# Adding attention's mask by four fp32 products in quarters of the TensorE array instead of two over the whole array, with a shorter planned step

## The chip, the cores and the metric

The kernel runs on one core of one Trainium2 chip. The metric is the device time of one execution in microseconds (us); lower is better. TensorE (PE) multiplies, VectorE (DVE) and ScalarE (ACT) work element by element, GpSimd (POOL) helps in attention, and SyncE (SP) issues the DMAs. Each engine takes its instructions strictly in the order in which the program emits them, so an instruction that waits holds up everything behind it on its engine.

## The reference

The kernel computes windowed attention and two gated layers behind it, all in fp32. Cut to what matters:

```python
# q, k, v: (4 batches, 8 heads, 576 positions, 64)
scores = (1.0 / np.sqrt(64)) * np.matmul(q, k.transpose(0, 1, 3, 2))
rel = pos[:, None] - pos[None, :]
mask = (rel >= 0) & (rel < 64)               # each query sees itself and the 63 before it
scores = np.where(mask, scores, -1e9)
attn = softmax(scores)
x = np.matmul(attn, v) -> (2304 tokens, 512)
# first layer: 512 -> 1536 -> 512
y = (silu(x @ w_gate) * (x @ w_val)) @ w_out
# second layer: 512 -> 1024 -> 1024 -> 512
out = (((y @ w1) * (y @ w2)) @ w3) @ w_out2
```

## The kernel before

**Attention** runs in 24 steps, m = 0 to 23, and three more that drain it. A step takes two groups i of three blocks each; a block is 64 queries of two heads against 128 keys. `emit_S` makes the scores of the step in two PSUM banks S, one for each i. It first adds the mask: one product over the whole 128x128 array for each i, a scaled identity `identr` times the mask, 384 columns wide, in fp32r (one pass over the array for each product). Then come the 12 score products (3 blocks, 2 groups, 2 heads), 64x64 with 128 columns, in fp32. Each of those uses a quarter of the array: the rows go by the head h, the columns by `place(i, h)`. An fp32 product that is not a transpose shows as two records in the trace. The product over all rows writes the bank first (`start=True`), the scores add to it.

In one step PE then does, in this order: the mask and the scores of step m (S), transposes of later q and k (T), the product with v of step m-3 (PV) and the transposes of the probabilities of step m-2 (PT). ACT does the exponentials (`pexp`) and copies, DVE the maxima, the sums' reciprocals and the copies of the transposed probabilities (`ptt`), POOL the division.

**What fills the gaps.** The gated layer behind attention works on fp32 numbers split into a high and a low fp32r part. The splitting is small jobs: unpack a weight tile (DVE L188, L190, L194, ACT L192), form sums and differences for a Strassen-like scheme of seven products (`combine`, DVE L208), copy the high part (`cast`, ACT L200) and subtract it for the low part (`rest`, DVE L204). The names `w_g` and `w_v` are the parts of the first tiles of w_gate and w_val, `xo_10` to `xo_71` those of attention's output X for its first 768 tokens (the first digit is the product 1 to 7, the second the half).

A `Plan` orders these jobs while the program is written out. It keeps a clock and, for each engine, the time at which that engine becomes free. In attention, `filling` charges each engine with what a step costs it (DVE 2.75, ACT 3.2, POOL 2.6 us) and moves the clock forward by a planned step of 3.85 us. Jobs that fit below the clock are emitted into DVE's order there, and into ACT's and SP's a little later in the step (`during_attention`). What does not fit stays queued. It is emitted after attention, as more time passes or when a product asks for it (`plan.need`, which emits what the product lacks, at once). The 24 planned steps are the only place where attention hands out time for these jobs.

**Behind attention** step 24 writes the first three products of the first gated unit: `ala` (product 1, needs `xo_10`, `xo_11`), `gaa` (product 2, needs `xo_20`, `xo_21`) and `bea` (product 5, needs `xo_50`, `xo_51`), between PT and the next PV. ACT copies `ala` out into `ha`, DVE adds `gaa` to it, ACT applies silu. Step 25 and 26 write two products each, beside the last PV.

Of the kernel before, what the change touches and what calls it, by code (L numbers as in the profile page):

```python
# [7 lines left out]
F32 = mybir.dt.float32  # L8
F32R = mybir.dt.float32r
# [7 lines left out]
P = 128  # L17
# [15 lines left out]
def window_attention_moe_kernel(ctx: ExitStack, tc: tile.TileContext, q, k, v, w_gate, w_val, w_out, w1, w2, w3, w_out2, out):  # L33
    nc = tc.nc
# [7 lines left out]
    SUB = 3  # L42
    NSUB = NJ // SUB
# [11 lines left out]
    own = ctx.enter_context(tc.tile_pool(name="own", bufs=1))  # L55
    ps = ctx.enter_context(tc.tile_pool(name="ps", bufs=8, space=PSUM))

    def bank(name):
        return ps.tile([P, 512], F32, tag="bank", name=name)

    def slot(shape, dtype, name, counted=True):

        plan.slots -= counted
        return sl.tile(shape, dtype, tag="s", name=name)
# [90 lines left out]
    plan = Plan()  # L155
# [83 lines left out]
    class Weights(Doubles):  # L239
# [12 lines left out]
        def place(self, p, x):  # L252
            if self.count % 3 == 0:
                self.tile = slot([P, 3, 2, P], F32R, f"w_{self.name}_{p}{'hl'[x]}")
            self.ops[p, x] = self.tile[:, self.count % 3]
            self.count += 1
            return self.ops[p, x]
# [71 lines left out]
    def x_tile(tp, c):  # L329
        if (tp, c) not in X:  # L330
            X[tp, c] = slot([P, TP], F32, f"X{tp}_{c}")
        return X[tp, c]

    def attention(events, filling):
        if True:
            ident, identr = own.tile([P, P], F32, name="ident"), own.tile([P, P], F32R, name="identr")
            masktiles = [slot([P, 2, SUB, P], F32R, f"mask{x}", False) for x in range(2)]
            mask = [masktiles[0][:, 0], masktiles[0][:, 1], masktiles[1][:, 0]]

            units = [(b, pr) for b in range(B) for pr in range(PAIRS)]  # L340
# [2 lines left out]
            raw, vt, qT, kT, sc, pexp, ptp, ptt, stat = {}, {}, {}, {}, {}, {}, {}, {}, {}  # L343
# [50 lines left out]
            def place(n, h):  # L394


                return (h + n) % 2

            def emit_S(m):
                both = (2 * m, 2 * m + 1)  # L400
                for i in both:
                    sc[i] = bank(f"S{i}")[:, :SUB * P].rearrange("p (j k) -> p j k", j=SUB)
                    nc.tensor.matmul(sc[i], lhsT=identr, rhs=mask[i % NSUB], start=True, stop=False)
                for jj in range(SUB):
                    for i in both:
                        u, s = divmod(i, NSUB)
                        j = SUB * s + jj
                        keys = kT[u].rearrange("p (w n) -> p w n", n=64)

                        keys = keys[:, :2] if j == 0 else keys[:, j - 1:j + 1] if j % 2 else keys[:, j - 1:j + 1][:, ::-1]  # L410
                        for h in range(2):
                            r, c = 64 * h, 64 * place(i, h)
                            nc.tensor.matmul(sc[i][c:c + 64, jj, :], lhsT=qT[u][r:r + 64, 64 * j:64 * j + 64],  # L413
                                             rhs=keys[r:r + 64], start=False,
                                             stop=jj == SUB - 1)
# [100 lines left out]
            for m in range(NM + 3):  # L516

                u0, r = 2 * (m // 3), m % 3
# [9 lines left out]
                if m < NM:  # L528
                    emit_S(m)
# [15 lines left out]
                for x in parts:  # L545
                    evac_T(*x)

                filling(m, NM)
                if 1 <= m <= NM:
                    emit_norm(m - 1)  # L550
# [621 lines left out]
    def filling(m, NM):  # L1172
        if m < NM:
            for e, cost in (("DVE", 2.75), ("ACT", 3.2), ("POOL", 2.6)):
                plan.charge(e, cost)
            plan.advance(3.85, ("ACT", "POOL", "SP"))

    with tc.manual_schedule():
        plan.shut.add("POOL")
        attention(during_attention, filling)  # L1180
        plan.slots += ATTENTION
        plan.ahead = 1.0
        for _ in gate:
            pass
        for _ in project(rows, wos, events_p):
            pass
        on(events2, len(order2) - 6, lambda: make_to(w3s[-1]))
        begin_e, run_e = final(rows2)

        def put_all():  # L1190
            for j in by:
                plan.need(j)
            begin_e()
        on(events2, len(order2) - 4, put_all)
        for _ in gated(xop2, left2, order2, AF.Copy, h2d, events2):
            pass
        run_e()
# [30 lines left out]
```

## Time and profile before

| | |
|---|---|
| median of 3 runs | 848.73 us (847.08 to 850.55) |
| the profiled execution's own time | 848.98 us |
| its span, first to last instruction | 847.3 us |
| PE busy in the span | 822.9 us, 97% |
| attention: masks of steps 0 to 23 start at | 7.6 to 94.6 us |
| DVE busy, ACT busy, 44.02 to 91.50 us | 46.69 and 47.43 of 47.48 us |

The profile is of one execution. The clock column (PEclk) is the share of TensorE's full 2.4 GHz that was granted. A row of the timeline gives the start, the duration of the merged instructions together, the engine, line, operation and tiles, the count, and in brackets the idle time before it with what ended it. Starts are more reliable than ends on PE, whose ends are modelled, so the pace of PE is read here from one start to the next.

### The profile page before, as it was taken

Reading aid. Unit: us, or ns where it says so; the run is one execution under the profiler, and the core shown is the slowest. Engines: PE = TensorE matmul, PEld = TensorE weight load, DVE = VectorE, ACT = ScalarE, POOL = GpSimd, SP = SyncE. Lnnn points to the kernel's source line nnn. Section 1 sums busy time; section 2 is a strip of 40 time slices with the busy share of each in tenths; the row PEclk is TensorE's granted clock in tenths of the full one; section 3 lists DMA queues with packets and bytes.
Section 4 is the critical chain, followed back from the end, with each engine's and each line's share of the span. In section 5 each row is a group of like instructions: output and inputs, shape, how many; then the busy total and the mean of one; then the engine's idle time right before and its main releaser. Section 6 shows DMA issues by size and latency. Waiting matters only on the chain.

```text
span 847.3 us, 15757 instructions
## 1 busy us (share of the span) xinstructions
PE 822.9 (97%) x5870; PEld 791.6 (93%) x5870; DVE 642.5 (76%) x1364; ACT 451.2 (53%) x1188; POOL 60.8 (7%) x89
## 2 busy tenths in 40 slices
PE   7899878899999999999999999999999999999998
PEld 6688767899999999999999999999999998899998
DVE  4799779878688767976698585778788844788884
ACT  6799855564646464643563362544444423766452
POOL 3467600000000000000000000000000000000000
PEclk9999999999999999999999999999999999999999
DMA  9989200135255324689996851015555329623522
GB/s 203 219 174 211 72 1 38 46 121 189 97 207 191 142 91 162 224 301 385 374 307 183 227 200 50 1 75 161 149 167 170 121 83 353 214 78 124 173 75 75
DMA packets 147516, 136.29 MB, mean 161 GB/s; under 512 B 95088, under 2 KB 114288, under 8 KB 146416
## 3 DMA queue, kind: packets, MB, share of 16 engines
q1 hardware_dynamic: 147440, 135.29, 51.0%
q8 instruction: 46, 0.75, 0.4%
q14 instruction: 30, 0.25, 0.1%
HBM read 92.27 MB, written 42.99 MB: 160 GB/s over the span
## 4 chain that ended last, share of the span: by engine, by line
PE 80%; DMA 7%; DVE 4%; SPq 4%; ACT 4%; issue 1%; ACTq 0%; DVEq 0%
PE ala L583 14%; PE alb L583 13%; PE o L723 12%; PE beb L583 7%; PE bea L583 7%; PE al L947 6%; PE acc L881 5%; PE gaa L583 3%; PE gab L583 3%; PE be L947 3%; DMA wo<-wo 2%; SPq L350 2%; PE PV L466 2%; PE ga L947 2%; ACT pexp L427 1%; PE PT L446 1%
## 5 line engine op out<-in xcount | busy, mean ns | idle before, releaser
L723 PE MATMUL o<-ph,wo 128*128 128x384 f32 x576 | 146.7, 334 | 0.2 <-DVE X L710 0.2
L723 PEld LDWEIGHTS o<-ph,wo 128*128 128x128 f32 x576 | 104.2, 188 | 0.5 <-DVE X L710 0.5
L723 PE MATMUL o<-pl,wo 128*128 128x384 f32 x288 | 96.3, 334 | 0.1
L590 ACT COPY ha<-ala 128x384 f32<-128x384 f32 x90 | 42.7, 478 | 57.6 <-PE ala L583 51.2
L594 DVE TENSOR_TENSOR ha<-ha,bea 128x384 f32<-128x384 f32 x60 | 33.2, 553 | 35.8 <-PE bea L583 19.9
L723 PEld LDWEIGHTS o<-pl,wo 128*128 128x128 f32 x288 | 54.1, 188 | 0.4 <-DVE pl L204 0.4
L427 ACT ACTIVATE pexp<-S,stat 128x128 f32<-128x128 f32 x144 | 53.8, 432 | 0.0
L604 ACT ACTIVATE ha<-ha 128x384 f32<-128x384 f32 x54 | 28.3, 526 | 39.1 <-DVE ha L594 39.1
L204 DVE TENSOR_TENSOR hf<-h,hf 128x384 fp32r<-128x384 f32 x84 | 43.5, 553 | 5.6 <-ACT hf L200 5.6
L200 ACT CAST ph<-pl 128x768 fp32r<-128x768 f32 x36 | 29.2, 836 | 34.4 <-DMA pl<-h 27.7
L200 ACT CAST hf<-h 128x384 fp32r<-128x384 f32 x84 | 39.3, 513 | 13.0 <-DVE h L208 11.4
L204 DVE TENSOR_TENSOR pl<-pl,ph 128x768 fp32r<-128x768 f32 x36 | 33.5, 952 | 13.0 <-ACT ph L200 12.5
L437 POOL TENSOR_TENSOR pexp<-pexp,stat 128x384 f32<-128x384 f32 x48 | 38.7, 826 | 41.7 <-DVE stat L434 37.2
L590 ACT COPY c12b<-alb 128x384 f32<-128x384 f32 x30 | 14.4, 480 | 49.4 <-PE alb L583 49.3
L427 ACT ACTIVATION_READ_ACCUMULATOR pexp<-S,stat 128x1 f32 x144 | 38.3, 270 | 0.0
L594 DVE TENSOR_TENSOR c22b<-c22b,beb 128x384 f32<-128x384 f32 x30 | 16.6, 555 | 27.1 <-ACT c22b L590 27.0
L583 PE MATMUL ala<-xo,w_g_6l 128*128 128x384 f32 x90 | 29.6, 338 | 1.6 <-ACT xo L200 1.0
L420 DVE TENSOR_REDUCE stat<-S 128x3 f32<-128x384 f32 x48 | 24.4, 551 | 7.4 <-PE S L413 7.2
L583 PE MATMUL ala<-xo,w_g_1h 128*128 128x384 f32 x120 | 27.7, 345 | 1.7 <-ACT w_g_1h L200 1.7
L466 PE MATMUL PV<-ptt,v 128*64 128x64 f32 x576 | 22.8, 229 | 5.1 <-DVE ptt L452 2.3
L917 ACT COPY o<-al 128x256 f32<-128x256 f32 x36 | 13.4, 373 | 27.0 <-PE al L947 26.0
L466 PEld LDWEIGHTS PV<-ptt,v 128*64 128x64 f32 x576 | 19.5, 139 | 8.8 <-issue 3.8
(533 smaller groups left out, 2490.2 us busy)
## 6 DMA issues: line engine op xcount, KB each, us to landing
h<-ha SPq DMA_DIRECT2D x60, 384.0 KB, 3.2
pl<-h SPq DMA_DIRECT2D x36, 384.0 KB, 6.4
h<-h SPq DMA_DIRECT2D x24, 384.0 KB, 4.9
st_w<-in_moe_w_dram SPq DMA_DIRECT2D x8, 1024.0 KB, 6.3
st_g<-in_moe_w_gate_dram SPq DMA_DIRECT2D x6, 1024.0 KB, 6.3
st_v<-in_moe_w_val_dram SPq DMA_DIRECT2D x6, 1024.0 KB, 5.5
st_wo<-in_moe_w_out_dram SPq DMA_DIRECT2D x6, 1024.0 KB, 5.4
wo<-by_wo SPq DMA_DIRECT2D x12, 512.0 KB, 3.7
```

The source lines that it names most:

```text
L200: (eng.copy if eng is nc.scalar else eng.tensor_copy)(out=hi(), in_=src())
L204: return plan.job(lambda eng: eng.tensor_tensor(out=lo(), in0=src(), in1=hi().bitcast(F32), op=ALU.subtract), after, slots=slots, DVE=dve( ...
L427: nc.scalar.activation(out=pe[:, jj, :], in_=so[:, jj, :], func=AF.Exp, bias=st[:, 0, x, jj:jj + 1], accum_out=st[:, 1, x, jj:jj + 1])
L437: nc.gpsimd.tensor_tensor(out=pe, in0=pe, in1=st[:, 3, x, :].unsqueeze(2).to_broadcast([P, SUB, P]), op=ALU.mult)
L466: nc.tensor.matmul(pp[64 * h:64 * h + 64, 64 * (SUB * x + jj):64 * (SUB * x + jj) + 64], lhsT=vt[u][e][:, at, h, :], rhs=t[:, x, jj, c:c + ...
L583: nc.tensor.matmul(acc, lhsT=self.wt.ops[p, x][:, m, :], rhs=self.xs.ops[p, m][:, y, :], start=start and n == 0, stop=n == 5, skip_group_c ...
L590: nc.scalar.copy(out=out, in_=src)
L594: nc.vector.tensor_tensor(out=out, in0=x, in1=y, op=ALU.add)
L604: nc.scalar.activation(out=h, in_=src, func=func)
L723: nc.tensor.matmul(acc[m, x], lhsT=wos.tiles[i // 6][:, i % 6, :], rhs=rows[2 * tp + x].words(f, b), start=f == n == 0, stop=f == NF - 1 a ...
L881: nc.tensor.matmul(acc, lhsT=w3T[i][c // 3][:, x, (c % 3) * P:(c % 3) * P + P], rhs=zt[c, y], start=c == k == 0, stop=c == NI - 1 and k == 2)
L947: nc.tensor.matmul(acc, lhsT=self.xs.ops[p, m][:, x, t * P:t * P + P], rhs=right.ops[p, m, y], start=start and n == 0, stop=n == 3 * R - 1 ...
```

## The change

The mask is kept in fp32, and it is added by products of 64x64 in the same quarters as the scores: four for each step, two for each i, of 384 columns each. The planned step goes from 3.85 to 3.55 us; the charges of the engines stay.

```diff
-            ident, identr = own.tile([P, P], F32, name="ident"), own.tile([P, P], F32R, name="identr")
-            masktiles = [slot([P, 2, SUB, P], F32R, f"mask{x}", False) for x in range(2)]
+            ident, identr = own.tile([P, P], F32, name="ident"), own.tile([P, P], F32, name="identr")
+            masktiles = [slot([P, 2, SUB, P], F32, f"mask{x}", False) for x in range(2)]
...
                 for i in both:
                     sc[i] = bank(f"S{i}")[:, :SUB * P].rearrange("p (j k) -> p j k", j=SUB)
-                    nc.tensor.matmul(sc[i], lhsT=identr, rhs=mask[i % NSUB], start=True, stop=False)
+                for i in both:
+                    for h in range(2):
+                        r, c = 64 * h, 64 * place(i, h)
+                        nc.tensor.matmul(sc[i][c:c + 64], lhsT=identr[r:r + 64, r:r + 64], rhs=mask[i % NSUB][r:r + 64],
+                                         start=True, stop=False)
...
-            plan.advance(3.85, ("ACT", "POOL", "SP"))
+            plan.advance(3.55, ("ACT", "POOL", "SP"))
```

PE's order in one step in the middle of attention, before, from the last probability transposes to the first transposes of q (S_1221 and S_1223 are the two score banks, a count behind a row is the number of products):

```order
L446 MATMUL PT_1186<-ident,pexp_1098 128x128 x3
L403 MATMUL S_1221<-mask_131,identr 128x384
L403 MATMUL S_1223<-mask_130,identr 128x384
L413 MATMUL S_1221<-kT_1105,qT_1019 64x128 x2
L413 MATMUL S_1223<-kT_1198,qT_1108 64x128 x2
L413 MATMUL S_1221<-kT_1105,qT_1019 64x128 x2
L413 MATMUL S_1223<-kT_1198,qT_1108 64x128 x2
L413 MATMUL S_1221<-kT_1105,qT_1019 64x128 x2
L413 MATMUL S_1223<-kT_1198,qT_1108 64x128 x2
L376 MATMUL T_0_1240<-ident,rawq_1040 128x96 x3
```

The same place of the change (line numbers behind the edit are four higher):

```order
L450 MATMUL PT_1200<-ident,pexp_1111 128x128 x3
L406 MATMUL S_1231<-mask_131,identr 64x384 x2
L406 MATMUL S_1232<-mask_130,identr 64x384 x2
L417 MATMUL S_1231<-kT_1118,qT_1032 64x128 x2
L417 MATMUL S_1232<-kT_1212,qT_1121 64x128 x2
L417 MATMUL S_1231<-kT_1118,qT_1032 64x128 x2
L417 MATMUL S_1232<-kT_1212,qT_1121 64x128 x2
L417 MATMUL S_1231<-kT_1118,qT_1032 64x128 x2
L417 MATMUL S_1232<-kT_1212,qT_1121 64x128 x2
L376 MATMUL T_0_1252<-ident,rawq_1051 128x96 x3
```

The two whole-array products have become four of a quarter; nothing else of PE's order differs in attention.

ACT's order at the end of attention, before, from the last exponentials (the pexp rows) over the table load to the copies of the next PV:

```order
L200 CAST xo_31_2101<-X_3_776 128x384
L427 ACTIVATE pexp_2127,stat_2084<-S_2042,stat_2084 128x128 x3
L542 ACT_TABLE_LOAD
L542 ACTIVATE masks<-masks 128x1
L480 COPY X_2_1801<-PV_2106 128x384
L590 COPY ha_0_0_2137<-ala_0_2139 128x384
L604 ACTIVATE ha_0_0_2137<-ha_0_0_2137 128x384
L483 COPY X_2_1801<-PV_2168 128x192
```

And of the change, from the copy of X behind the table load to the same copy of PV:

```order
L484 COPY X_2_1810<-PV_2114 128x384
L200 CAST xo_10_2148<-X_0_455 128x384
L200 CAST xo_11_2151<-X_1_537 128x384
L594 COPY ha_0_0_2145<-ala_0_2147 128x384
L200 CAST w_v_6h<-st_v_461 128x256 x2
L200 CAST xo_20_2168<-X_2_709 128x384
L200 CAST xo_21_2171<-X_3_789 128x384
L608 ACTIVATE ha_0_0_2145<-ha_0_0_2145 128x384
L200 CAST w_v_6h<-st_v_461 128x256
L200 CAST w_v_6l<-st_v_461 128x256
L200 CAST xo_50_2188<-X_0_455 128x384
L200 CAST xo_51_2191<-X_1_537 128x384
```

Ten casts that stood among the steps of attention now stand here: two ahead of the copy of `ala`, four between it and silu, four behind silu.

DVE's order at the same place, before, from the last reciprocal of attention to the first copy of transposed probabilities behind it:

```order
L434 RECIPROCAL stat_2084<-stat_2084 128x6
L594 TENSOR_TENSOR ha_0_0_2137<-ha_0_0_2137,gaa_0_2147 128x384
L208 TENSOR_TENSOR X_1_528<-X_3_776,X_1_528 128x384
L208 TENSOR_TENSOR X_0_447<-X_2_698,X_0_447 128x384
L452 COPY ptt_2165<-PT_2119 128x384
```

And of the change, from the subtraction for xo_20 on:

```order
L204 TENSOR_TENSOR xo_20_2168<-X_2_709,xo_20_2168 128x384
L204 TENSOR_TENSOR xo_21_2171<-X_3_789,xo_21_2171 128x384
L598 TENSOR_TENSOR ha_0_0_2145<-ha_0_0_2145,gaa_0_2167 128x384
L204 TENSOR_TENSOR w_v_6l<-st_v_461,w_v_6h 128x256 x2
L204 TENSOR_TENSOR xo_50_2188<-X_0_455,xo_50_2188 128x384
L204 TENSOR_TENSOR xo_51_2191<-X_1_537,xo_51_2191 128x384
L204 TENSOR_TENSOR w_v_4l<-st_v_461,w_v_6h 128x256
L208 TENSOR_TENSOR X_0_455<-X_2_709,X_0_455 128x384
L208 TENSOR_TENSOR X_1_537<-X_3_789,X_1_537 128x384
L456 COPY ptt_2204<-PT_2127 128x384
```

Between the last reciprocal and the addition of `gaa` stand seven jobs where none stood (the five ahead of this piece are xo_10, xo_11, a part of w_v and two combinations), and between that addition and the copy of `ptt` seven where two stood. Further on the orders of all engines meet again after three more subtractions on DVE (for w_v_4l, xo_30 and xo_31) and two casts on ACT, and from there they are the same to the end. On SP two rows move: one load for later weights (`st_g`) goes behind ten later rows of loads of q, k and v, the other (`st_v`) to the end of attention's loads. On DVE the first unpacking of `st_v` (L188) stands one step later.

## Rows read from the trace of the kernel before

**Rows 1.** The page, head and part 1: the span, and PE's busy time and share.

```profile
span 847.3 us, 15757 instructions
PE 822.9 (97%) x5870; PEld 791.6 (93%) x5870; DVE 642.5 (76%) x1364; ACT 451.2 (53%) x1188; POOL 60.8 (7%) x89
```

**Rows 2.** Windows: length, busy of PE, PEld, DVE, ACT, POOL; then clock, DMA, GB/s.

```profile
44.02:91.50 47.48, 47.48 (x837) 39.48 (x835) 46.69 (x118) 47.43 (x223) 32.52 (x44) 1.00 0.88 189
96.00:118.00 22.00, 16.53 (x159) 14.48 (x159) 12.59 (x28) 11.11 (x37) 7.06 (x10) 0.92 0.01 1
118.00:165.00 47.00, 39.97 (x217) 37.01 (x216) 40.89 (x86) 28.16 (x65) 0.00 (x0) 1.00 0.09 34
200.00:700.00 500.00, 499.18 (x2876) 498.06 (x2876) 379.08 (x759) 234.41 (x485) 0.00 (x0) 1.00 0.52 176
```

**Rows 3.** Timeline of PE over one step in mid-attention.

```profile
61.65 0.87 PE L446 MATMUL PT<-ident,pexp 128*128 128x128 f32 x6
62.28 0.60 PE L403 MATMUL S<-mask,identr 128*128 128x384 f32 x2
62.81 0.89 PE L413 MATMUL S<-kT,qT 64*64 64x128 f32 x24
63.63 0.71 PE L376 MATMUL T<-ident,rawk 96*128 96x96 f32 x6
64.52 0.92 PE L466 MATMUL PV<-ptt,v 128*64 128x64 f32 x24
66.00 0.42 PE L403 MATMUL S<-mask,identr 128*128 128x384 f32 x1
```

**Rows 4.** Timeline of the weight loads (PEld) in the same step.

```profile
62.81 0.64 PEld L413 LDWEIGHTS S<-kT,qT 64*64 64x64 f32 x24 [0.25 <-issue]
63.62 0.53 PEld L376 LDWEIGHTS T<-ident,rawk 96*128 96x128 f32 x6 [0.17 <-issue]
```

**Rows 5.** Timeline of PE in stretches 0.035 us long, at 62.97 and at 63.08.

```profile
62.81 0.45 PE L413 MATMUL S<-kT,qT 64*64 64x128 f32 x8
62.81 0.56 PE L413 MATMUL S<-kT,qT 64*64 64x128 f32 x12
```

**Rows 6.** Timeline of PE in the gated layer: fp32r products of 384 columns.

```profile
136.02 1.20 PE L583 MATMUL beb<-xo,w_v_5h 128*128 128x384 f32 x6
137.06 1.20 PE L583 MATMUL alb<-xo,w_v_6h 128*128 128x384 f32 x6
```

**Rows 7.** Timeline of PE in attention's first half: its three waits.

```profile
24.28 0.36 PE L376 MATMUL T<-ident,rawq 96*128 96x96 f32 x2 [2.02 <-DMA rawq<-in_q_dram]
34.45 1.03 PE L466 MATMUL PV<-ptt,v 128*64 128x64 f32 x24 [0.50 <-DVE ptt L452]
38.75 0.94 PE L466 MATMUL PV<-ptt,v 128*64 128x64 f32 x24 [0.58 <-ACT pexp L427]
```

**Rows 8.** Timeline of DVE there.

```profile
33.23 0.43 DVE L188 TENSOR_SCALAR st_v<-st_v 128x512 int32<-128x512 int32 x1 [1.78 <-DMA st_v<-in_moe_w_val_dram]
```

**Rows 9.** Timeline of PE at the end of attention and behind it.

```profile
94.59 0.60 PE L403 MATMUL S<-mask,identr 128*128 128x384 f32 x2
95.11 0.89 PE L413 MATMUL S<-kT,qT 64*64 64x128 f32 x24
102.32 2.06 PE L583 MATMUL ala<-xo,w_g_1h 128*128 128x384 f32 x6
104.22 0.51 PE L583 MATMUL gaa<-xo,w_g_1h 128*128 128x384 f32 x2
107.63 0.94 PE L466 MATMUL PV<-ptt,v 128*64 128x64 f32 x24 [1.17 <-DVE ptt L452]
```

**Rows 10.** Timeline of ACT at the same place.

```profile
101.50 0.46 ACT L480 COPY X<-PV 128x384 f32<-128x384 f32 x1
104.41 0.48 ACT L590 COPY ha<-ala 128x384 f32<-128x384 f32 x1 [2.46 <-PE ala L583]
```

**Rows 11.** Timeline of DVE at the same place.

```profile
105.53 0.55 DVE L594 TENSOR_TENSOR ha<-ha,gaa 128x384 f32<-128x384 f32 x1 [4.82 <-PE gaa L583]
106.93 1.01 DVE L452 COPY ptt<-PT 128x384 f32<-128x384 f32 x2
```

**Rows 12.** Timeline in the gated layer: casts in a row, subtractions in a row.

```profile
131.37 3.00 ACT L200 CAST xo<-X 128x384 fp32r<-128x384 f32 x7
118.93 1.96 DVE L204 TENSOR_TENSOR xo<-X,xo 128x384 fp32r<-128x384 f32 x4
```

## The prediction

> **What bounds the kernel now.** I read the page first: PE is busy for 97% of the span [rows 1]. Next the windows by stage [rows 2]: from 200 us on PE runs without a gap worth naming (499.18 of 500 us), so whatever the first 165 us lose or win comes out at the end unchanged; nothing behind it can take it up. That leaves two stretches. In mid-attention, 44.02 to 91.50 us, PE is busy for all of the 47.48 us, but DVE and ACT are at 98% and 100% too, so the share alone doesn't say who sets the step. The timeline does: in a whole step [rows 3] no PE row has an idle time, and PE's weight loads wait only for "issue" [rows 4], which is PE changing its tiling and no other engine. So the step is PE's: masks start at 62.28 and 66.00, and over the 13 steps from 44.02 to 91.50 the mean is 3.65 us. The second stretch, 96 to 165 us, is the other way round: PE is idle for 5.5 us of 22 and 7.0 us of 47 [rows 2], and the waits name ACT and DVE [rows 9 to 11].
>
> **The mask on PE.** From start to start, the two fp32r products take 0.53 us, the scores 0.82 [rows 3]. Of the first, 0.25 is the change of tiling ahead of the scores, of the second 0.17 is the change ahead of T [rows 4]; so scores alone stream for 0.65 us. They are 12 products of 128 columns, 1536 columns in fp32, each in a quarter. The new mask is 4 products of 384 columns: the same 1536 columns, type and quarters, with the same order over the quarters. Does all of that run four abreast? In two stretches 0.11 us apart the records begun since 62.81 are 8 and 12 [rows 5]: four records start every 0.107 us, one for each quarter, and 0.107 us is 128 columns at two clocks each at 2.4 GHz. So I price the mask at 0.64 us. Cross-check of the old one: six fp32r products of 384 columns take 1.04 us from start to start [rows 6], 0.17 each, so two stream for 0.35 and the rest of the 0.53 is the switch. A switch is not saved: scores follow the mask without one, but the mask now follows the probability transposes (whole array, 61.65 to 62.28 [rows 3]) with one, which I take at 0.17. New block: 0.17 + 0.64 = 0.81 against 0.53, **+0.28 us a step**. Bounds: if a record in a quarter streamed one column a clock, as fp32r does, the mask would take 0.32 + 0.17 = 0.49 (-0.04); if only two quarters ran at once, 1.28 + 0.17 = 1.45 (+0.92). The scores are the nearest row by far (same type, same quarters), so I take the middle value.
>
> The Trainium skill speaks against that ("TensorEngine Tiling (Array Packing)", Restrictions and Gotchas, Gotcha 1): different row tiles cannot access one PSUM bank at the same time. By that rule the two heads of a group i, which sit in different row halves and write one S bank, would take turns, and the price would be the +0.92 above. The trace disagrees: the score products of [rows 5] have just this layout and start in fours.
>
> **Where the 0.28 lands.** Steps 0 to 4: nothing; the transposes of step 4 wait 2.02 us for a load of q that lands at 24.28 whatever PE does [rows 7], more than 5 x 0.28. Steps 5 to 8 (27.1 to 44.0 us): +1.1 us on PE, but PE has two waits there, 0.50 for DVE's `ptt` and 0.58 that the profile gives to ACT [rows 7]. The first goes back to DVE standing 1.78 us at L188 for the load of `st_v` [rows 8], with `ptt` behind it. The change puts L188 a step later, and puts less filler on both engines, so I count both waits as gone: +0.1 in all (bounds 0 and +1.1). The 13 steps to 91.50: 13 x 0.28 = +3.6; DVE and ACT, which might be next to bind, carry less per step than before. The last step before the final scores is 94.59 - 91.50 = 3.09 us long [rows 2, 9], where PE has about 2.85 to do, so it grows by 0.04, and the last mask adds 0.28. **Attention: +4.0 us** (bounds +3 and +5.2).
>
> **The work put off.** The shorter planned step takes 24 x 0.30 = 7.2 us of planned time from the jobs. In the orders, ten casts and twelve DVE jobs more than before now stand between the last exponentials and the copy of `ptt` that PV of step 25 needs. A row of casts runs at 0.42 us each (seven in 3.00, the last 0.51), a row of subtractions at 0.47 (four in 1.96) [rows 12]. I use before's times; attention's +4.0 comes on top.
> - ACT copies X at 101.50 in both [rows 10], as the last exponentials and the table load are not moved. `xo_10` then starts at 101.92 and ends at 102.43, `xo_11` at 102.85; DVE's low parts follow at 103.0 and 103.45. `ala` started at 102.32 and took 1.90 to the next start [rows 9], slow; it now starts at 102.45 and meets its low parts on the way, so it ends about 0.1 late, and ACT copies it at 104.5 instead of 104.41.
> - ACT then casts two parts of w_v, `xo_20` and `xo_21` before anything else: `xo_20` is there at 104.5 + 3 x 0.42 + 0.51 = 106.3, `xo_21` at 106.7, low parts at 106.8 and 107.25. `gaa`, which ran at 104.22 without a wait, now ends near 107.6, and DVE adds it at 107.8 instead of 105.53 [rows 11]: +2.2.
> - silu on ACT waits for that addition, and behind silu wait two more casts of w_v, `xo_50` and `xo_51`. Silu starts at 108.35; `xo_50` is there at 108.35 + 3 x 0.42 + 0.51 = 110.1, `xo_51` at 110.55, the low parts at 110.65 and 111.1. `bea` needs them and ends near 111.6.
> - DVE, at its low part of `xo_51` until 111.1, has a part of w_v and two combinations (3 x 0.47 less overlap, 1.3) ahead of `ptt`, which so starts near 112.3, against 106.93. PV of step 25, which waited for `ptt` until 107.63 [rows 9, 11], starts near 113.0: **+5.3 us**. Bounds: +4.5 if the 256-column casts of w_v are quicker than the 0.42 of the 384-column ones; +7 if PE, idle between those products, gets the low clock for `gaa` and `bea` as well (`ala` shows it: 0.32 for each product against 0.17 in [rows 6]).
>
> From there PE, ACT and DVE have the old order again, with three more subtractions on DVE (1.4 us) and two more casts on ACT (0.8) before 128 us. DVE is idle for 6.1 of 47 us there [rows 2] and takes part of it; PE waits for both engines, so I take +0.7 (bounds 0 and 1.4). The moved loads cost nothing: they are weights for the second set of tiles, whose L188 is not in attention, and no load of attention is queued behind `st_v`.
>
> **The sum**: 4.0 + 5.3 + 0.7 = +10.0 us on the profiled execution's 848.98 us (span 847.3 and 1.7 around it), 0.25 above the median: 859.0 us, 1.2% more.
>
> **The rivals.**
> 1. Quarters cost no more than the whole array. For it: the low bound of the mask, which no fp32 row here reaches; against: [rows 5]. Attention then gives -0.04 x 18 steps and the two waits, -1.7 in all, the rest stays: 848.98 - 1.7 + 6.0 = 853.3.
> 2. Only two quarters at once. For it: the page's rule; against: the scores. 18 x 0.92 - 1.0 = +15.6 and 6.0: 870.6.
> 3. Faster: DVE and ACT set the step, not PE. At 98% and 100% busy they might, if PE's back-to-back starts only follow their pace. Each step would then shed the 0.30 us of jobs that the plan no longer puts in: 18 x 0.30 = -5.4. The put-off jobs cost nothing if they fit into the idle time behind attention: DVE has 22 - 12.59 = 9.4 us of it, ACT 10.9 [rows 2], for some 5 us each. That gives 843.6. It decides only from the point where PE has a gap in each step that the longer mask can use; [rows 3, 4] show none, and the put-off jobs stand in a chain with PE, not beside it.
>
> **How the numbers follow.** Forecast 0.77, with its own range from its bounds, +7.5 to +13.6: 856.5 to 862.6. Rival 1 0.10, rival 2 0.06, rival 3 0.07. A change under 0.5% (4.2 us) can't be told from none by this measurement. Faster: rival 3 mostly, 0.06. Same: most of the rest of rival 3, half of rival 1, 0.07. Slower: 0.87. The range, 853.2 to 864, holds the forecast with some room above for a longer low clock and nearly all of rival 1's upper half.
>
> **What would show it.** Right: in mid-attention the scores start 0.64 us behind the mask, and masks stand 3.93 us apart in the mean instead of 3.65, with an "issue" idle ahead of the mask's weight loads and none ahead of the scores'; DVE and ACT idle in attention; PE waits on ACT's `xo_20` and `xo_50` casts behind attention, `ptt` of step 25 about 5 us later after the last scores; from 200 us on the same rows, shifted by 10. Wrong: masks under 3.7 or over 4.2 us apart (the price of a quarter), or `gaa` starting without a wait (the chain behind silu).

## The result, and the profile after

| | before | after |
|---|---|---|
| median of 4 runs each | 849.13 us (847.08 to 850.55) | 862.01 us (861.46 to 863.58) |
| ratio, 95% interval | | 1.0142 (1.0111 to 1.0172) |
| the profiled execution's own time, span | 848.98, 847.3 us | 862.04, 860.3 us |

The change costs 12.9 us; 859.0 was forecast, with 853.2 to 864.0 as the range. The page's head and part 1 and the windows of the changed kernel, which answer [rows 1, 2]:

```profile
span 860.3 us, 16045 instructions
PE 834.2 (97%) x6014; PEld 795.0 (92%) x6014; DVE 641.3 (75%) x1364; ACT 454.1 (53%) x1188; POOL 59.1 (7%) x89
```

```profile
43.16:94.26 51.10, 51.10 (x913) 39.91 (x912) 39.97 (x108) 46.13 (x214) 31.41 (x44) 1.00 0.78 169
96.00:118.00 22.00, 14.41 (x158) 10.52 (x156) 15.70 (x35) 12.95 (x48) 7.59 (x11) 0.79 0.00 1
118.00:165.00 47.00, 40.03 (x220) 36.21 (x218) 36.98 (x76) 25.94 (x60) 0.00 (x0) 0.92 0.12 40
200.00:700.00 500.00, 500.00 (x2886) 499.88 (x2885) 384.38 (x771) 239.64 (x495) 0.00 (x0) 1.00 0.53 179
```

PE has no gap in these 13 steps of attention, as before, and none from 200 to 700 us, where it had 0.82 us of them [rows 2]; DVE and ACT now have idle time in attention (39.97 and 46.13 of 51.10). New is the clock column: 0.79 and 0.92 in the two stretches behind attention, 0.92 and 1.00 before. One step of PE in mid-attention, and its weight loads, for [rows 3, 4]:

```profile
61.89 0.87 PE L450 MATMUL PT<-ident,pexp 128*128 128x128 f32 x6
62.70 0.88 PE L406 MATMUL S<-mask,identr 64*64 64x384 f32 x8
63.39 0.83 PE L417 MATMUL S<-kT,qT 64*64 64x128 f32 x24
64.16 0.71 PE L376 MATMUL T<-ident,rawk 96*128 96x96 f32 x6
66.70 0.55 PE L406 MATMUL S<-mask,identr 64*64 64x384 f32 x4
```

```profile
62.70 0.21 PEld L406 LDWEIGHTS S<-mask,identr 64*64 64x64 f32 x8 [0.17 <-ACT X L487]
63.07 0.15 PEld L417 LDWEIGHTS S<-kT,qT 64*64 64x64 f32 x4 [0.17 <-issue]
```

From start to start the mask takes 0.69 us (its four products show as 8 records, two each), the transposes ahead of it 0.81, where they took 0.63, and the scores behind it 0.77, where they took 0.82. PE behind attention, which answers [rows 9]:

```profile
98.07 0.83 PE L417 MATMUL S<-kT,qT 64*64 64x128 f32 x24
105.04 0.44 PE L587 MATMUL ala<-xo,w_g_1h 128*128 128x384 f32 x1 [1.10 <-ACT xo L200]
109.27 1.28 PE L587 MATMUL gaa<-xo,w_g_1h 128*128 128x384 f32 x2 [1.61 <-ACT xo L200]
114.07 2.56 PE L587 MATMUL bea<-xo,w_g_2l 128*128 128x384 f32 x6 [2.24 <-ACT xo L200]
116.96 1.55 PE L470 MATMUL PV<-ptt,v 128*64 128x64 f32 x24 [0.33 <-DVE ptt L456]
```

ACT and DVE at the same place, for [rows 10, 11]:

```profile
107.69 0.48 ACT L594 COPY ha<-ala 128x384 f32<-128x384 f32 x1 [2.29 <-PE ala L587]
108.70 0.92 ACT L200 CAST xo<-X 128x384 fp32r<-128x384 f32 x2
112.45 0.52 ACT L608 ACTIVATE ha<-ha 128x384 f32<-128x384 f32 x1 [2.83 <-DVE ha L598]
113.51 0.92 ACT L200 CAST xo<-X 128x384 fp32r<-128x384 f32 x2
```

```profile
109.25 1.03 DVE L204 TENSOR_TENSOR xo<-X,xo 128x384 fp32r<-128x384 f32 x2 [0.99 <-ACT xo L200]
111.86 0.55 DVE L598 TENSOR_TENSOR ha<-ha,gaa 128x384 f32<-128x384 f32 x1 [1.59 <-PE gaa L587]
116.26 1.01 DVE L456 COPY ptt<-PT 128x384 f32<-128x384 f32 x2
```

PE now waits for the casts ahead of `ala`, `gaa` and `bea`, and four windows of the changed kernel show what else is new there:

```profile
110.00:112.00 2.00, 1.82 (x5) 1.31 (x5) 0.41 (x2) 0.00 (x0) 0.00 (x0) 0.50 0.00 0
114.00:116.00 2.00, 1.93 (x5) 1.63 (x6) 1.95 (x5) 0.43 (x2) 0.00 (x0) 0.50 0.00 0
126.00:128.00 2.00, 2.00 (x8) 2.00 (x7) 0.00 (x0) 0.48 (x1) 0.00 (x0) 0.50 0.00 0
143.00:146.00 3.00, 3.00 (x11) 3.00 (x11) 1.97 (x5) 2.41 (x6) 0.00 (x0) 0.50 0.00 0
```

The granted clock is 0.50 (1.2 of 2.4 GHz) in three stretches that follow waits of PE, the first of which the first two windows show; in it the six products of `bea` are busy for 2.56 us where six such products have 1.20 in [rows 6].

Where the 12.9 us lie, by landmarks on PE's timeline of both kernels: the last scores start 2.96 later (95.11 to 98.07); from there to PV of step 25 it takes 18.89 us where it took 12.52, +6.37; from there to `ala` of the seventh unit (the one that waits for ACT's `w_g_1h`) 56.21 where it took 51.71, +4.50. The rows of that `ala`, before and after:

```profile
159.34 1.44 PE L583 MATMUL ala<-xo,w_g_1h 128*128 128x384 f32 x6 [1.73 <-ACT w_g_1h L200]
173.17 1.44 PE L587 MATMUL ala<-xo,w_g_1h 128*128 128x384 f32 x6 [1.71 <-ACT w_g_1h L200]
```

The three add up to 13.83; the spans differ by 13.0, since PE's 0.82 us of gaps from 200 to 700 us are gone. The forecast had 4.0, 5.3 and 0.7.

### The profile page after: what moved, and what is told of

Read it like the earlier page. It is cut to its first block, busy times and chain, and to the rows that moved or that the text cites. A ratio compares the mean times of both kernels' runs of the same rounds, so it can differ in the third digit from the quotient of the medians.

```text
span 860.3 us, 16045 instructions
## 1 busy us (share of the span) xinstructions
PE 834.2 (97%) x6014; PEld 795.0 (92%) x6014; DVE 641.3 (75%) x1364; ACT 454.1 (53%) x1188; POOL 59.1 (7%) x89
## 4 chain that ended last, share of the span: by engine, by line
PE 88%; SPq 3%; DVE 3%; DMA 3%; ACT 2%; issue 1%; DVEq 0%; ACTq 0%
PE o L727 17%; PE ala L587 14%; PE alb L587 13%; PE beb L587 7%; PE bea L587 7%; PE al L951 6%; PE acc L885 5%; PE gab L587 4%; PE gaa L587 3%; PE be L951 3%; PE PV L470 2%; SPq L350 2%; PE ga L951 2%; PE S L406 1%; PE PT L450 1%; PE T L376 1%
## 5 line engine op out<-in xcount | busy, mean ns | idle before, releaser
L431 ACT ACTIVATE pexp<-S,stat 128x128 f32<-128x128 f32 x144 | 51.8, 394 | 0.0
L431 ACT ACTIVATION_READ_ACCUMULATOR pexp<-S,stat 128x1 f32 x144 | 33.5, 233 | 0.0
L204 DVE TENSOR_TENSOR xo<-X,xo 128x384 fp32r<-128x384 f32 x42 | 22.6, 574 | 8.9 <-ACT xo L200 8.9
L417 PEld LDWEIGHTS S<-kT,qT 64*64 64x64 f32 x576 | 18.9, 137 | 8.5 <-issue 7.3
L587 PEld LDWEIGHTS ala<-xo,w_g_1h 128*128 128x128 f32 x120 | 21.1, 188 | 5.7 <-DVE xo L204 2.1
```

The costliest lines, as they stand in the source:

```text
L204: return plan.job(lambda eng: eng.tensor_tensor(out=lo(), in0=src(), in1=hi().bitcast(F32), op=ALU.subtract), after, slots=slots, DVE=dve( ...
L431: nc.scalar.activation(out=pe[:, jj, :], in_=so[:, jj, :], func=AF.Exp, bias=st[:, 0, x, jj:jj + 1], accum_out=st[:, 1, x, jj:jj + 1])
L587: nc.tensor.matmul(acc, lhsT=self.wt.ops[p, x][:, m, :], rhs=self.xs.ops[p, m][:, y, :], start=start and n == 0, stop=n == 5, skip_group_c ...
```

## The experiments

Each kernel ran beside the kernel before on the same chip. The last three were on a chip where that one took 851.02 us instead of some 849.8, so the ratio is what compares.

| run | mask | planned step | median us | before, same chip | ratio (95%) |
|---|---|---|---|---|---|
| e1_mask_alone | fp32, quarters | 3.85 | 857.19 | 849.90 | 1.0077 (1.0051 to 1.0104) |
| e2_step_alone | fp32r, whole | 3.55 | 856.61 | 849.90 | 1.0079 (1.0058 to 1.0101) |
| e5_quarters_bf16 | bf16, quarters | 3.85 | 850.38 | 849.90 | 1.0000 (0.9982 to 1.0018) |
| e7_busy_gaps | fp32, quarters | 3.55 | 862.70 | 849.90 | 1.0156 (1.0132 to 1.0181) |
| e8_step_370 | fp32r, whole | 3.70 | 851.34 | 849.62 | 1.0021 (1.0003 to 1.0038) |
| e9_busy_gaps2 | fp32, quarters | 3.55 | 858.81 | 849.62 | 1.0116 (1.0093 to 1.0140) |
| e10_before_busy | fp32r, whole | 3.85 | 848.11 | 849.62 | 0.9978 (0.9962 to 0.9993) |
| e11_bf16_380_busy | bf16, quarters | 3.80 | 847.99 | 849.62 | 0.9986 (0.9970 to 1.0001) |
| e12_x_first | fp32, quarters | 3.55 | 865.35 | 851.02 | 1.0181 (1.0152 to 1.0210) |
| e13_mask_alone_busy | fp32, quarters | 3.85 | 854.26 | 851.02 | 1.0040 (1.0021 to 1.0058) |
| e14_step_alone_busy | fp32r, whole | 3.55 | 857.20 | 851.02 | 1.0074 (1.0052 to 1.0097) |

**Mask alone and step alone.** The first is the change without its last line, the second is the kernel before with that line:

```diff
-            plan.advance(3.85, ("ACT", "POOL", "SP"))
+            plan.advance(3.55, ("ACT", "POOL", "SP"))
```

> The four fp32 products in quarters, with the planned step left at 3.85 us. By the theory on record the mask makes PE's step 0.28 us longer (3.65 to 3.93 us over the 13 steps of mid-attention, +3.6), the last mask adds 0.28, steps 5 to 8 up to 1.1, and the orders behind attention stay as before: +4 to +5 us, 853 to 854. If the whole loss were the mask's, 862; if it were the plan's alone, 849.

> The planned step of 3.55 us, with the two fp32r products kept. By the theory PE's step stays at 3.65 us (attention shorter by 1 us at most, from the waits of the first half), the put-off jobs cost some 6 us up to the PV of step 25, and the low clock and later waits some 3 more: +8 to +9, 857 to 858. If the whole loss were the mask's, 849. If DVE and ACT set the step of before, 18 steps give back 0.30 us each and the time is near 852.

The two losses, 0.77% and 0.79%, add up to that of the change, 1.42%, within their intervals. So both halves lose, each by about the same. The step alone lost 6.7 us by its median, a little under its expectation of 8 to 9. PE's timeline of the mask alone, the scores of steps 9 and 23:

```profile
44.75 0.83 PE L417 MATMUL S<-kT,qT 64*64 64x128 f32 x24
98.97 0.83 PE L417 MATMUL S<-kT,qT 64*64 64x128 f32 x24
```

And of the step alone:

```profile
44.71 0.89 PE L413 MATMUL S<-kT,qT 64*64 64x128 f32 x24
94.73 0.89 PE L413 MATMUL S<-kT,qT 64*64 64x128 f32 x24
113.99 1.55 PE L466 MATMUL PV<-ptt,v 128*64 128x64 f32 x24 [0.33 <-DVE ptt L452]
```

From the scores of step 9 to those of step 23 it is 54.22 us with the quarters, 50.02 without, where before has 50.57 (44.54 to 95.11). All six runs with fp32 quarters give 54.21 or 54.22, with either planned step: the mask's price there is 3.65 us against the kernel before, and 4.20 against the step alone. A step given 0.30 us less filler is shorter by 0.04 us in the mean (0.55 in 14 steps, half of it in the last), so the third rival (DVE and ACT set the step) falls. What is put off shows in the last row: 19.26 us from the last scores to PV of step 25, against 12.52, with the mask of before.

The mask alone was over its expectation by its median (+7.3 us against 4 to 5); its interval, +4.3 to +8.8, still reaches into it. Its profiled execution took 854.24 us, which is as expected, and shows one place where more comes from. Two rows of its PE timeline behind attention and the windows over them, then the same products of the kernel before:

```profile
134.25 2.12 PE L587 MATMUL alb<-xo,w_v_4h 128*128 128x384 f32 x6
136.17 1.84 PE L587 MATMUL beb<-xo,w_v_3h 128*128 128x384 f32 x6
```

```profile
134.00:136.00 2.00, 2.00 (x9) 2.00 (x8) 1.59 (x4) 1.52 (x4) 0.00 (x0) 0.53 0.00 0
136.00:138.00 2.00, 2.00 (x9) 2.00 (x8) 1.02 (x2) 1.85 (x5) 0.00 (x0) 0.61 0.00 0
```

```profile
130.79 1.23 PE L583 MATMUL alb<-xo,w_v_4h 128*128 128x384 f32 x6
131.86 1.20 PE L583 MATMUL beb<-xo,w_v_3h 128*128 128x384 f32 x6
```

The order and the waits ahead of them are the same in both (1.67 and 1.11 us against 1.67 and 1.12); in the one the clock is 0.53 and 0.61 over 4 us behind them, in the other 1.00 from 130 to 134 us.

**Is it the quarters or fp32's passes?** The mask in bf16, in the same quarters, with the planned step of before:

```diff
-NEG_A, NEG_B = 3125.0, -320000.0
+NEG_A, NEG_B = 32768.0, -32768.0
...
-            ident, identr = own.tile([P, P], F32, name="ident"), own.tile([P, P], F32, name="identr")
-            masktiles = [slot([P, 2, SUB, P], F32, f"mask{x}", False) for x in range(2)]
+            ident, identr = own.tile([P, P], F32, name="ident"), own.tile([P, P], mybir.dt.bfloat16, name="identr")
+            masktiles = [slot([P, 2, SUB, P], mybir.dt.bfloat16, f"mask{x}", False) for x in range(2)]
```

> The mask in the same four quarters, but in bf16 (factors 32768 and -32768 in place of 3125 and -320000), with the planned step at 3.85 us. If what the quarters cost is fp32's passes, four quarters abreast stream 384 columns once, 0.16 us; with the change of tiling, 0.17, the block takes 0.33 instead of 0.81, PE has 3.45 us of work in a step, and DVE and ACT (3.59 and 3.65 us busy in a step of before) become the bound: a step of about 3.6 us, 848 us. If PE alone set the step, 18 x 0.2 us less: 845.5. If it is the quarters that are dear, whatever the type, 853 to 854 as with the mask alone.

PE's timeline in mid-attention, and the 13 steps as a window:

```profile
62.44 0.36 PE L406 MATMUL S<-mask,identr 64*64 64x384 bf16 x4
62.62 0.82 PE L417 MATMUL S<-kT,qT 64*64 64x128 f32 x24
```

```profile
44.26:91.35 47.09, 45.73 (x861) 37.52 (x861) 46.46 (x118) 46.99 (x223) 32.52 (x45) 1.00 0.87 194
```

Half the records, and 0.18 us from the mask to the scores instead of 0.69: the quarters are cheap, fp32's passes are dear. Yet the step is 3.62 us, not 3.45: PE now has gaps, and DVE and ACT are at 46.46 and 46.99 of 47.09. In the kernel before, PE's step of 3.65 and theirs of 3.62 lie almost on each other. A longer mask costs nearly its whole length there, a shorter one gives next to nothing (0.03 us a step).

**Does the low clock cost what the forecast lacked?** The change with further products of 384 columns, overwritten by the product behind them, as work for PE in its waits. The first such run had them ahead of `gaa` and `bea`:

```diff
+                for _ in range({2: 8, 5: 12}.get(p, 0) if self.n == 0 else 0):
+                    nc.tensor.matmul(acc, lhsT=self.wt.ops[1, 0][:, 0, :], rhs=self.xs.ops[1, 0][:, 0, :],
+                                     start=True, stop=True)
```

> The change as it is, with 8 further fp32r products of 384 columns ahead of gaa and 12 ahead of bea, into the same banks and overwritten by gaa and bea: work for PE in its waits for the casts, 1.4 and 2.1 us of it. If the idle time brings the low clock, and that is what the forecast lacked, gaa and bea take 1.04 us instead of 1.9 to 2.5 each, PV of step 25 starts some 2 us earlier and the time is 858 to 860. If the low clock costs nothing, since ACT and DVE set the pace there, the time stays at 862; if the added products stand in the way, it is above.

The time says no. But the edit also put its 20 products into the second gated layer, where PE has no wait (its rows at 544.91 and 547.34): 20 x 0.174 = 3.5 us of plain loss. And its scores of step 9 began 1.97 us later than in the change, which has the same orders, with a load of q that PE waited for until 25.42 instead of 23.93. Its way from PV of step 25 to `ala` of the seventh unit is 52.52 us, against 56.21. So the edit was made again for the first layer alone:

```diff
-        hs = {}
+        hs, recent = {}, []
...
+                for _ in range({(0, 2): 4, (0, 5): 12, (2, 5): 9, (4, 5): 6, (6, 1): 8}.get((self.n, p), 0) if func == AF.Silu else 0):
+                    nc.tensor.matmul(acc, lhsT=recent[0], rhs=recent[1], start=True, stop=True)
+                recent[:] = self.wt.ops[p, 0][:, 0, :], self.xs.ops[p, 0][:, 0, :]
```

> The change as it is, with further fp32r products of 384 columns ahead of five products of the first gated layer whose operands come late: 4 ahead of gaa, 12 ahead of bea (both of the first unit), 9, 6 and 8 ahead of bea of the third and fifth unit and ala of the seventh; each is overwritten by the product behind it, and unlike in the run before none stands in the second layer. If the low clock behind attention is what the forecast lacked, it comes back: 2.5 to 4 us less than the change, 858 to 859.5, and the way from PV of step 25 to ala of the seventh unit is about 0.8 us longer than in before instead of 4.5. If ACT and DVE set the pace whatever the clock, 861.5 to 863.

858.81 us, as expected. PE's timeline (L586 are the further products), and windows of the same run:

```profile
106.85 0.88 PE L586 MATMUL gaa<-xo,w_g_1h 128*128 128x384 f32 x4
108.63 0.44 PE L590 MATMUL gaa<-xo,w_g_1h 128*128 128x384 f32 x1 [0.90 <-ACT xo L200]
110.20 2.27 PE L586 MATMUL bea<-xo,w_g_1h 128*128 128x384 f32 x12
112.62 1.73 PE L590 MATMUL bea<-xo,w_g_2l 128*128 128x384 f32 x6
115.52 0.94 PE L470 MATMUL PV<-ptt,v 128*64 128x64 f32 x24 [1.17 <-DVE ptt L456]
```

```profile
110.00:112.00 2.00, 2.00 (x14) 2.00 (x13) 1.23 (x3) 1.01 (x3) 0.00 (x0) 1.00 0.00 0
120.00:130.00 10.00, 8.23 (x64) 7.42 (x63) 7.05 (x15) 6.13 (x14) 0.00 (x0) 1.00 0.15 37
130.00:165.00 35.00, 32.30 (x177) 30.20 (x177) 31.83 (x67) 19.76 (x45) 0.00 (x0) 1.00 0.17 65
```

In this execution the clock is at 1.00 throughout. From the last scores (97.43) to PV of step 25 it takes 18.09 us instead of 18.89, and from there to `ala` of the seventh unit 52.49 instead of 56.21: 0.8 and 3.7 us. That is what the low clock cost in the change's profiled execution. What the further products bring in the mean is less well known: the ratio went from 1.0142 to 1.0116, some 2.2 us, and the two intervals overlap. The profiled execution is the fastest of the six (856.97 us); the others, at a mean granted clock of 0.992 to 0.996, took 857.06 to 862.54, where the four of the change had 0.988 to 0.990.

The kernel before with the same edit and `{(2, 5): 8, (4, 5): 5, (6, 1): 8}`:

> The kernel before, with 8, 5 and 8 further products ahead of bea of the third and fifth unit and ala of the seventh, in its waits of 1.67, 1.08 and 1.73 us. If these waits bring the low clock in some executions and not in others, the times of one kernel lie closer together than the 5 us of before and the median falls by 1 to 2: 847.5 to 849. If the clock there is nothing to the time, 849.5 to 850.

848.11 us, 0.22% less than before (0.07 to 0.38%), and its 12 times lie within 4.0 us (845.56 to 849.53), where the 29 of before beside it span 7.4. The mean granted clock of the 12 is 0.995 to 1.000, that of the 29 is 0.987 to 0.998. Its trace doesn't show the gain where the products stand: the clock is 0.50 from 128 to 130 us, behind the wait of 1.12 us that follows the first of them, and from PV of step 25 to `ala` of the seventh unit it takes 53.26 us, 1.55 more than in before. What was better in that execution lies ahead of them (`ala` of the first unit at full clock, step 9 begun 1.44 us earlier). So the gain by the products rests on the times and the mean clocks alone. With mask or step alone the edit was tried on another chip:

> The four quarters alone (planned step 3.85) with 8, 5 and 8 further products in the same three waits as in the kernel before with further products, 848.1. With the clock held up there, what is left between the two is the mask's price in attention: 3.8 to 4.1, so 852. If the mask alone brings more than its 0.28 a step, as the 6.6 us of the run without further products might say, 854 to 855.

> The planned step of 3.55 with the mask of before, and the further products of the second run of the change with them (4, 12, 9, 6 and 8): the fourth corner. If mask and step add up with the clock held, it is 858.8 - 4.0 = 854.8, which is 6.7 above the kernel before with further products; if the two cost more together than apart, over 856.

The mask alone went from 1.0077 to 1.0040, with intervals that overlap, and the step alone stayed (1.0079 and 1.0074). The clock was not held in either trace: with the mask alone it is 0.57 from 134 to 138 us, with the step alone 0.50 from 100 to 108, having fallen ahead of the first of the further products. Both expectations gave times by e10's chip; on this one before is 1.4 us slower, so the ratios are compared. Against e10, the mask then costs 0.62% and the step 0.96%, with intervals of some 0.3 points on either side, too wide to decide between 4 and 5 us; their sum, 1.58%, is no less than the 1.38% of both together (e9), so nothing says that the two cost more together than apart. The rows of the mask alone again say 54.21.

**Does a job cost by its number or by its place?** Half the shortening, with the mask of before (`plan.advance(3.70, ...)`):

> The mask of before with a planned step of 3.70 us, half of the way to 3.55. In ACT's order xo_21 then stands behind the copy of ala, and xo_50 and xo_51 behind silu; the casts for xo_10, xo_11, xo_20 and the parts of w_v stay ahead. By the chain of the forecast gaa waits for xo_21 (1.0 us later), silu goes with it, xo_51 ends about 1.4 us behind silu and ptt of step 25 some 2.5 to 3 us later than in before: 852 to 853, attention itself unchanged. If a late job costs only once the first product lacks its operands (xo_10, xo_11), 849.5 to 850. If attention's step follows DVE and ACT, 18 x 0.15 us less: 847.

1.8 us, less than expected. `ala` ran at full clock in its profiled execution, and PV of step 25 is 13.78 us behind the last scores. Against the 12.52 of before, whose `ala` was slow, that is 1.3; against the 11.05 of e10, whose `ala` also had the full clock (100.13 to 101.27), it is the 2.7 that the chain gives; attention gives back 0.36 (50.21 from the scores of step 9 to those of step 23). Then X's jobs were put ahead of the weights':

```diff
+                plan.rank = -1 if tp == 0 else 0
                 xop1[tp] = Operands([X[tp, c] for c in range(KC)], f"xo{tp}")
+                plan.rank = 0
```

> The change with one line more: the jobs for X's first operands (xo_10 to xo_31) go ahead of the weights' jobs in the plan's queue, so that casts of X are done in attention and parts of w_g_6, w_v_1 and w_v_2 are put off in their place. As many jobs are late as in the change, but gaa and bea, and with them ptt of step 25, wait for none. If the loss is the chain through those casts, PV of step 25 stands some 12.5 us behind the last scores as in before (18.9 in the change); the parts of w_v are wanted by alb right behind it, some 2 to 3 us of waits come back there, and the time is 857 to 859. If only the number of late jobs counts, 861 to 863.

Right in the first half and wrong in the second. Its PE timeline:

```profile
108.96 0.94 PE L470 MATMUL PV<-ptt,v 128*64 128x64 f32 x24 [1.17 <-DVE ptt L456]
115.41 2.29 PE L587 MATMUL alb<-xo,w_v_1h 128*128 128x384 f32 x6 [3.12 <-ACT w_v_1h L200]
124.73 1.01 PE L587 MATMUL gab<-xo,w_v_1h 128*128 128x384 f32 x2 [3.43 <-ACT w_v_1h L200]
129.04 1.33 PE L587 MATMUL beb<-xo,w_v_2l 128*128 128x384 f32 x3 [2.03 <-ACT w_v_2l L200]
```

With no cast in the way, PV of step 25 stands 10.28 us behind the last scores (98.68) instead of 18.89: the chain through the casts is what held it. But the weights that are late instead need unpacking on DVE and ACT in turn before their casts, and cost 8.6 us of waits in three places, with the clock at 0.50 from 124 to 130 us between them; 3.3 us more in all than the change.

**A version that beats both?** The bf16 mask with a planned step of 3.80 and further products:

> The mask by four bf16 products in quarters (0.18 us from mask to scores in the run with 3.85 us), the planned step at 3.80, at which no cast of xo_1 to xo_5 stands behind attention, and the same further products ahead of the three late ones. PE then has 3.45 us of work in a step, and DVE and ACT set it; they are given 0.05 us less in each: 18 x 0.05, 0.9 us off the bf16 run, and 1 to 2 from the clock: 847 to 848.5. If PE's share of the step still sets it, 18 x 0.2 less than before: 845 to 846.5. If neither counts, 850.

847.99 us, 1.6 less than before, with an interval that just reaches 1. The time is in the expected range, but the shorter step that it was to come from isn't shown: in its profiled execution masks stand 3.74 us apart from step 9 to 22, with a wait of 1.84 us for a load of q and a lower clock behind it. It can't be told from e10, whose mask is that of before. Both are faster than before by less than the 0.5% that the prediction set as its bound; only e10's interval lies clear of 1.

## Why the prediction was right, by its steps

**PE sets the step, and the mask costs 0.28 more: right.** Masks stand 3.93 us apart (43.16 to 94.26 in 13 steps), as forecast; the mask takes 0.69 where 0.64 was priced, the switch ahead of it 0.18 (0.81 less 0.63) where 0.17 was, and the scores are 0.05 shorter, so 0.28 came out partly because two errors of 0.05 cancel. From step 9 to 23 the price is 3.65 us in six runs, against 3.6 + 0.04 forecast. The rule of the Trainium skill ("TensorEngine Tiling (Array Packing)", Restrictions and Gotchas, Gotcha 1: row tiles can't access one PSUM bank at the same time) would have made the mask 1.28; 0.69, and 0.18 in bf16, disagree. Three small things in the prediction were wrong, without a price: the weight loads' idle time ahead of the mask stands under ACT's copy, and the scores' loads still show 0.17 under "issue"; the switch ahead of the scores was read as 0.25, while the cross-check of the old mask leaves 0.18; and in the first rival's sum 18 x 0.04 and the two waits make 1.8, not 1.7.

**Attention +4.0: +2.96 in this pair.** The difference lies ahead of step 9, whose scores began at 43.85 instead of 44.54. It can't be laid to the change: with the same orders e7 began them at 45.82 and e9 at 43.22. Loads of q that land earlier or later move this by more than 2 us from one execution to the next, with PE's waits of 0.48 and 0.76 us for them in the change's timeline in place of [rows 7].

**The work put off +5.3: +6.37.** The chain stands as forecast. Counted from the last scores, the forecast has `xo_20` ready 11.19 us behind them, and `gaa` starts 11.20 behind; in e9, with the clock at 1.00, PV follows at 18.09 where the forecast has 17.89. Of the 1.07 that were missing, 0.8 is the low clock in `gaa` and `bea`, which the prediction had as its upper bound (+7).

**Later +0.7: +4.5.** This is the term that was mis-sized. The orders cost what was forecast: e7 and e9, with the clock up, need 0.81 and 0.78 us more than before on this way. The rest, 3.7, is the low clock. The run e7 shows it best, as it has the change's order there and no further products; its two ends of this way:

```profile
118.76 0.94 PE L470 MATMUL PV<-ptt,v 128*64 128x64 f32 x24 [1.16 <-DVE ptt L456]
171.28 1.46 PE L590 MATMUL ala<-xo,w_g_1h 128*128 128x384 f32 x6 [1.71 <-ACT w_g_1h L200]
```

Row by row the change falls behind it by 0.6 us in PV and PT of step 25, by 1.56 from 125.6 to 129.2 us and by 1.56 from 142.1 to 146.7, which are the stretches with the clock at 0.50, and nowhere else by more than 0.04. The prediction took the low clock for something that can strike `gaa` and `bea`, and gave it no place behind them, though PE waits there as well, in before too. That the sum came within 3 us is in part luck: the first term was 1.04 too high and the 0.82 of gaps went away, against 1.07 and 3.8 too low.

**The rivals.** The first two (a quarter no dearer; only two quarters at once) fall with 0.69 and 54.21. The third falls with e2, but less widely than the prediction had it: DVE and ACT are 0.03 us behind PE in a step (e5), so "PE's back-to-back starts only follow their pace" was nearly true.

**What stays open.** Why the clock falls behind one wait and not behind the same wait in another execution, and how far further products prevent it. The 29 executions of before that ran beside e8 to e11 show its size: ten with a mean granted clock of 0.996 or more took 846.3 to 850.3 us, eight with 0.991 or less 851.4 to 853.7. The Trainium skill ("TensorE: Matmul & The Clock Gate", Part 1) has the gate look at PE's activity in windows that run freely and don't restart with a kernel; the scatter agrees with that, but no run here shows the windows.

## What to carry to other kernels

Price an instruction on the array by its passes and columns, read from a row of the same type and tiling, not by the share of the array that it covers: here four quarter products in fp32 (0.69 us) cost more than two whole ones in fp32r (0.35). Time that a planner doesn't hand out doesn't vanish: its jobs come due between instructions that wait for one another, and putting other jobs off instead can be worse, so follow the chain of each one to PE. And where a change makes PE wait, allow for the clock in the work behind each wait, over the whole stretch in which PE is not yet without gaps.

## What the runs showed of the hardware that was not expected

- Two DVE subtractions of 128x384 took 1.96 us in the change (from 105.02), while POOL divided; four of them took that without it [rows 12].
- An fp32 mask product of 64x64 shows as two records, the bf16 one as one, and the block of four goes from 0.69 to 0.18 us, by nearly four.
- With the same order of PE's products there, the granted clock behind PE waits of 1.7 and 1.1 us was 0.53 and 0.61 in one execution (e1) and 1.00 in another (before), worth some 1.5 us at one place. With products that nobody uses put ahead of three late ones, the kernel before was 0.22% faster (0.07 to 0.38%) at a higher mean clock, though its one trace still has 0.50 behind one of its waits.
